# A fixed order for every operation, and layer 1's result kept in DRAM, in an attention kernel with two feed-forward layers

## The chip, the cores and the metric

The kernel runs on one core of a Trainium2 chip, as one program in one launch. The metric is the device time of that program in microseconds (us), lower is better. The kernel before takes 837.86 us (median of 3 runs, 836.62 to 838.67). The profile shown here is of one further execution, which took 837.84 us.

## The reference

```python
def _attn_ref(q, k, v):                      # (4, 8, 576, 64) each
    scores = scale * q @ k^T                 # scale = 1/sqrt(64)
    mask_local   = (rel >= 0) & (rel < 32)                    # heads 0 to 3
    mask_strided = (rel >= 0) & (pos_k % 32 == pos_q % 32)    # heads 4 to 7
    scores = where(mask, scores, -1e9)
    attn = exp(scores - max); attn = attn / (sum(attn) + 1e-9)
    return attn @ v
def _moe_ref(x, w_in, w_out):                # w_in 512 x 2048, w_out 2048 x 512
    h = x @ w_in; g = maximum(0.01 * h, h); return g @ w_out
def _moe2_ref(x, w_in, w_out):
    h = x @ w_in; g = maximum(h, 0) + log1p(exp(-abs(h))); return g @ w_out
x = attn_out.transpose(0, 2, 1, 3).reshape(2304, 512)
return _moe2_ref(_moe_ref(x, w1_in, w1_out), w2_in, w2_out)
```

The four weights reach the kernel as 8-byte floats (2 MiB for a quarter of one), and the result has to be close to float32.

## The kernel before, in words

Both layers multiply in float16, with every operand split into a high and a low half: three products (`mm3`, L676 to L678) stand for one. A weight quarter is loaded with one DMA (L170) into one of four staging areas of `pair`, and then goes through a chain on the vector engine (DVE) and the scalar engine (ACT): largest value (L179), low words (L185), the sign (L224), a shift or scale (L230, L234), the join of two words (L245), high half (L253), low half (L260, on DVE for the first quarter of W1, on GpSimd, that is POOL, for its other three).

**Attention** goes by batch (b = 0 to 3) and six steps ("halves") of a batch: scores on TensorE (PE; `dots`, L397 to L409), maxima on DVE (L436, L447), exponentials on ACT (L477, L499), sums, a reciprocal, a product on POOL (L525), a transpose (on PE for batches 0 and 1, by a DMA, L579, for 2 and 3, followed by a join on DVE, L585), the product with v (L606, L611), and the split of the result into the halves of x (L660 to L672). The largest value of v (L327 or L338) is spread to all partitions by a tiny matmul (`over`, L142).

**Layer 1** goes by 8 units of 288 tokens (u = 0 to 7, two to a batch). `plan_first` makes the gated values g of a unit: 16 column tiles f of W1, each 12 matmuls of 288 columns (one tile is the unit of PE work in this text), then a bend and a split on ACT and POOL (L697 to L703). `plan_second` multiplies g with O1 (16 steps of 12 matmuls) and moves the result (`out_move`, L1080) to a buffer x2 in on-chip memory that holds all of layer 1's output, two arrays of `x2p`. The first unit goes by f (`plan_second_by_f`). The homes of g: `gtile` and `gtile3` are one buffer each; unit 6 and unit 7 both use `gtile`, so that unit 7's g can only be made when the second product of unit 6 is done.

**Layer 2** goes by 9 units of 256 tokens (class `Unit`): the largest value of the unit's x2, a factor, the split (`high`, `rest`), then 8 pairs k of column tiles: `first` (24 matmuls of 256 columns), `size`, `relu`, `soft` on ACT, `add` on POOL (L1421), `sums` on DVE (L1429), the split (`cut_high` L1433 on ACT, `cut_rest` L1437 on DVE) and `second` (21 matmuls; 7 products for 8 in the manner of Strassen). The unit's result is combined on DVE and stored. The O2 quarters, of which the differences are also needed (`o2_sums`, L1249), all go through staging area 1, one after the other.

**The order.** The program first lists 1800 and some operations with `plan.add(engine, cost, function, deps, rank, take, free, behind, port)`, and then `Plan.run` emits them. Each engine executes its own instructions in the order in which they are emitted, so an instruction that waits holds up all that stand behind it on its engine; the DMA triggers of the sync engine (SP) are such a queue too. `run` keeps a model clock for each engine. At each step it takes the engine with the earliest possible start, and of its operations that could start within SLACK the one with the lowest rank (table RANKS, a start and a slope for each kind of work). Buffers that several operations share are counted by name (`take`, `free`): two PSUM pairs "mm", one "sc", and so on. Where the model sees PE idle in the first 130 us, it puts filler matmuls (`idle`, L109) there.

Of the kernel before, what the change touches and what calls it, by code (L numbers as in the profile page):

```python
# [20 lines left out]
P = 128  # L21
# [24 lines left out]
RING = 5  # L46

RANKS = {
# [10 lines left out]
}  # L59
# [12 lines left out]
def build(tc, qt, kl, ks, v, wi1, wo1, wi2, wo2, mloc, mstr, msml, out):  # L72
    nc = tc.nc
    with ExitStack() as ctx:
# [14 lines left out]
        gp3 = pool("gp3", bufs=1)  # L89
        front = ctx.enter_context(ExitStack())  # L90
# [187 lines left out]
        class Attn:  # L278
            def __init__(self, b):

                self.b, self.mode, self.small = b, MODES[b], b in SMALL
                self.q, self.k = {}, {}
                self.ps, self.sm, self.st, self.sv, self.s = {}, {}, {}, {}, {}
                self.turned, self.hl = b in TURNED, {}
# [12 lines left out]
            def load_early(self):  # L297
                for p, masks in ((0, [(mn, msml)]), (1, [(ml, mloc), (ms, mstr)])):
# [4 lines left out]
                    for mask in masks:  # L303
                        nc.scalar.dma_start(*mask)
# [257 lines left out]
            def cut(self, half):  # L562
# [4 lines left out]
                self.cuts = [y[:r].rearrange("p (j n w) -> p j n w", j=2, n=n)[:, :, :, :w] for y in both]  # L567
                nc.scalar.activation(self.cuts[0], self.sv[half], AF.Copy)

            def remain(self, half):  # L570
                hi, lo = self.cuts
# [138 lines left out]
        class Op:  # L710
            def __init__(self, eng, cost, fn, deps, rank, take, free, behind, port):
# [3 lines left out]
                self.next, self.missing, self.end = [], 0, None  # L715

        class Plan:


            HOP, SLACK, LOAD = 0.2, 0.5, 2.6  # L720
# [15 lines left out]
            def run(self, order):  # L736
                rank = {o: order[o.rank[0]][0] + order[o.rank[0]][1] * o.rank[1] for o in self.ops}
# [3 lines left out]
                open_ = []  # L741
                for o in self.ops:
                    o.end, o.next, o.places = None, [], []
                for o in self.ops:
                    o.missing = len(o.deps) + len(o.behind)
                    for d in [*o.deps, *o.behind]:
                        d.next.append(o)
                    if not o.missing:
                        open_.append((0.0, o))
                left = len(self.ops)  # L750
                while left:
                    best = {}
                    for ready, o in open_:
                        t = max(ready, clock[o.eng], clock["port"] if o.port else 0.0)
                        want = collections.Counter()
                        for n in o.take:
# [467 lines left out]
        def part_homes(q):  # L1224
# [4 lines left out]
            if q == 1:  # L1229
                return one(a3, 1536), two(more(), 0)  # L1230
# [419 lines left out]
```

## Time and profile before

| | kernel before |
|---|---|
| median of 3 runs | 837.86 us (836.62 to 838.67) |
| profiled execution: its time, its span | 837.84 us, 835.9 us |
| PE busy | 817.7 us (98%) |
| DVE, ACT, POOL busy | 518.4, 523.6, 261.4 us |
| DMA read, written | 50.12 MB, 4.72 MB |

The span runs from the first to the last instruction of the profiled execution; the execution's own time is 1.9 us longer. In a timeline a row gives the start, the time, the engine (SPq is the DMA queue of SP), the line of the kernel, the operation, what it writes and reads, how many instructions were merged, and in brackets the idle time of the engine just before and the operation that ended it. A busy PE can be busy with fillers (L109), so its busy share alone does not tell how much of its work is needed.

### The profile page before, as it was taken

The page shows a single profiled execution, that of the slowest core. Times are in us where ns is not written, and L with a number is a line of the kernel's source. Part 1 is how long each engine was busy: PE and PEld are TensorE (multiplying, and loading weights), DVE is VectorE, ACT ScalarE, POOL GpSimd, SP SyncE. Part 2 cuts the span into 40 slices and gives each one's busy share as a digit, 9 for nine tenths or more (in the row PEclk, how much of TensorE's full clock was granted, in tenths as well). Part 3 has the DMA queues.
Part 4 walks back from the last instruction along what each step waited for, and adds up shares of the span by engine and source line. Part 5 has one row for each costly group of instructions (what it writes and reads, how often), then busy time and mean ns, then how long its engine had stood idle before and what let it go on. Part 6 is the DMA issues. An engine that isn't in the chain of part 4 may idle for free.

```text
span 835.9 us, 18197 instructions
## 1 busy us (share of the span) xinstructions
PE 817.7 (98%) x7622; PEld 676.4 (81%) x7622; DVE 518.4 (62%) x1198; ACT 523.6 (63%) x947; POOL 261.4 (31%) x193
## 2 busy tenths in 40 slices
PE   9998999899999999999999999999999999999997
PEld 5677777677777777777777878888888888888886
DVE  4999879731367134668448766657474746556564
ACT  1788889721457563336446389868677685959591
POOL 1237949730114431003214033313222231313231
PEclk9999999999999999999999999999999999999999
DMA  9952420420226103550220200000000000000000
GB/s 354 417 198 113 169 101 19 97 82 2 62 67 188 20 2 59 203 201 1 102 101 12 91 1 2 26 2 26 2 26 2 26 2 26 5 22 27 2 27 26
DMA packets 30595, 60.79 MB, mean 73 GB/s; under 512 B 20689, under 2 KB 22065, under 8 KB 27953
## 3 DMA queue, kind: packets, MB, share of 16 engines
q1 hardware_dynamic: 29824, 59.17, 21.1%
q8 instruction: 60, 0.98, 0.5%
q10 hardware_dynamic: 688, 0.46, 0.2%
q14 instruction: 23, 0.18, 0.1%
HBM read 50.12 MB, written 4.72 MB: 66 GB/s over the span
## 4 chain that ended last, share of the span: by engine, by line
PE 75%; DVE 15%; DMA 5%; ACT 3%; issue 1%; POOL 0%; SPq 0%; ACTq 0%; DVEq 0%; POOLq 0%
PE o L676 12%; PE o L678 12%; PE o L677 12%; PE h L676 11%; PE h L678 11%; PE h L677 11%; DVE pair L245 3%; DMA pair<-wo_dram 2%; DVE pair L234 1%; DVE m L179 1%; PE ps L409 1%; DVE pair L1249 1%; PE po L611 1%; DMA pair<-wi_dram 1%; DMA pair<-v_dram 1%; DVE s L447 1%
## 5 line engine op out<-in xcount | busy, mean ns | idle before, releaser
L676 PE MATMUL h<-x,w 128*128 128x256 f16 (+1 forms) x1088 | 303.6, 279 | 0.1
L678 PE MATMUL h<-x,w 128*128 128x256 f16 (+1 forms) x1088 | 303.4, 279 | 0.2 <-POOL w L260 0.2
L677 PE MATMUL h<-x,w 128*128 128x256 f16 (+1 forms) x1088 | 303.4, 279 | 0.0
L1421 POOL TENSOR_TENSOR pair<-pair,t 128x512 f32<-128x512 f32 x72 | 96.3, 1341 | 269.1 <-ACT pair L1409 147.9
L703 POOL TENSOR_TENSOR g<-t,g 128x576 f16<-128x576 f32 x64 | 107.8, 1692 | 150.6 <-ACT g L700 150.6
L676 PE MATMUL o<-g,pair 128*128 128x288 f16 x512 | 146.6, 286 | 0.0
L677 PE MATMUL o<-g,pair 128*128 128x288 f16 x512 | 146.4, 286 | 0.0
L678 PE MATMUL o<-g,pair 128*128 128x288 f16 x512 | 146.4, 286 | 0.0
L1437 DVE SCALAR_TENSOR_TENSOR gr<-pair,x2g,gr 128x896 f16<-128x896 f32 x72 | 87.2, 1221 | 69.1 <-ACT gr L1433 69.1
L676 PEld LDWEIGHTS <-w 128*128 128x128 f16 x1088 | 106.4, 98 | 19.9
L678 PEld LDWEIGHTS <-w 128*128 128x128 f16 x1088 | 106.4, 98 | 19.6 <-POOL w L260 0.5
L677 PEld LDWEIGHTS <-w 128*128 128x128 f16 x1088 | 106.5, 98 | 18.7
L1429 DVE TENSOR_TENSOR pair<-pair 128x128 f32<-128x128 f32 x288 | 72.8, 298 | 54.5 <-POOL pair L1421 51.7
L1404 ACT ACTIVATE t<-h,x2s 128x512 f32<-128x512 f32 x72 | 48.8, 678 | 60.1 <-PE h L678 58.9
L525 POOL TENSOR_TENSOR s<-s,sm 128x288 f32<-128x288 f32 (+6 forms) x48 | 45.0, 958 | 132.0 <-DVE sm L520 67.4
L1433 ACT ACTIVATE gr<-pair,x2g 128x896 f16<-128x896 f32 x72 | 73.7, 1034 | 14.9 <-DVE pair L1429 14.8
L697 ACT ACTIVATE t<-h,gs 128x576 f32<-128x576 f32 x64 | 47.1, 736 | 41.4 <-PE h L678 39.3
L676 PEld LDWEIGHTS <-pair 128*128 128x128 f16 x512 | 50.1, 98 | 14.3 <-issue 0.3
L678 PEld LDWEIGHTS <-pair 128*128 128x128 f16 x512 | 50.1, 98 | 12.6
L677 PEld LDWEIGHTS <-pair 128*128 128x128 f16 x512 | 50.1, 98 | 12.1
L676 PEld LDWEIGHTS <-gr 128*128 128x128 f16 x504 | 49.3, 98 | 7.0 <-ACT gr L1433 1.3
L676 PE MATMUL o<-pair,gr 128*128 128x256 f16 x198 | 54.0, 273 | 1.0 <-ACT gr L1433 1.0
(143 smaller groups left out, 1438.7 us busy)
## 6 DMA issues: line engine op xcount, KB each, us to landing
pair<-wi_dram SPq DMA_DIRECT2D x8, 2048.0 KB, 10.8
pair<-wo_dram SPq DMA_DIRECT2D x8, 2048.0 KB, 8.3
out_dram<-pair SPq DMA_DIRECT2D x18, 256.0 KB, 2.2
v<-v_dram SPq DMA_DIRECT2D x2, 1856.0 KB, 16.2
pair<-v_dram SPq DMA_DIRECT2D x2, 1408.0 KB, 7.1
q<-qt_dram SPq DMA_DIRECT2D x6, 288.0 KB, 5.8
k<-kl_dram SPq DMA_DIRECT2D x4, 304.0 KB, 3.5
q<-qt_dram SPq DMA_DIRECT2D x4, 298.0 KB, 6.4
```

The costliest lines, as they stand in the source:

```text
L245: nc.vector.scalar_tensor_tensor(out=f.rearrange("p (s n) -> p s n", s=2), in0=hi, scalar=3, in1=lo, op0=ALU.logical_shift_left, op1=ALU.b ...
L525: nc.gpsimd.tensor_tensor(out=sv, in0=sv, in1=rs, op=ALU.mult)
L676: nc.tensor.matmul(ps, ah, bh, start=first, stop=False)
L677: nc.tensor.matmul(ps, ah, bl, start=False, stop=False)
L678: nc.tensor.matmul(ps, al, bh, start=False, stop=last)
L697: nc.scalar.activation(t, ps, AF.Prelu, scale=gates[f // 4], alpha=0.01)
L703: nc.gpsimd.tensor_tensor(out=g[:, 1, f : f + 2, :], in0=t, in1=g[:, 0, f : f + 2, :], op=ALU.subtract)
L1404: nc.scalar.activation(t, self.ps[k], AF.Prelu, scale=self.sc[:, k // 2 : k // 2 + 1], alpha=-1.0)
L1421: nc.gpsimd.tensor_tensor(out=r, in0=r, in1=self.a[k], op=ALU.add)
L1429: nc.vector.tensor_tensor(out=r[:, o], in0=r[:, x], in1=r[:, y], op=op)
L1433: nc.scalar.activation(self.a[k][:, 0], self.r[k][:, 1:], AF.Copy, scale=self.ag[:, k // 2 : k // 2 + 1])
L1437: nc.vector.scalar_tensor_tensor(out=a[:, 1], in0=self.r[k][:, 1:], scalar=self.ag[:, k // 2 : k // 2 + 1], in1=a[:, 0], op0=ALU.mult, op1 ...
```

## The change

RANKS goes, and with it the choice in `run`: ORDER lists all 1834 operations by the number of their `plan.add` call, in the sequence in which they are emitted. The model clock stays, for the fillers alone. The numbers: 0 to 4 are batch 0's loads, 5 to 104 its attention; 105 to 109 and 110 to 210 the same of batch 1; 211 to 250 the quarters of W1 (10 each: load, largest, over, scale, low, sign, shift, join, high, rest); 251 to 285 O1; 286 to 445 g of units 0 to 3 (40 each, 5 to two tiles); 446 to 463 the second product of unit 0, 464 to 523 those of units 1 to 3 (20 each); 524 to 634 and 635 to 745 the loads and attention of batches 2 and 3; 746 to 985 units 4 to 7 (g and second product, 40 and 20 each); 986 the opening of a buffer; 987 to 1026 W2; 1027 to 1078 O2 (13 each); 1079 a join of scales; 1080 to 1833 the layer 2 units (83 each but the last: load, largest, over, factor, high, rest, scales, then 9 for each k, then move, two combines, store).

Layer 1's result goes through DRAM: `out_move` writes to a small tile "t" (shared with the gates of both layers), a DMA stores it (16 DMAs), and each layer 2 unit loads its 256 tokens back into one of four slots of the first x2 array (9 DMAs). The second x2 array now holds parts of O2 (`more`), in place of `gtile3`, and unit 7's g moves to `gtile3`, so that it only waits for unit 5's second product. The second product of unit 6 accumulates in "sc". The ring `rs` moves to the places of two W1 tiles. The first `first` of layer 2 waits for the second product of unit 6, no more for that of unit 7. Batch 0's first mask is triggered on SP after the two first loads of q, no more between the two loads of k on ACT's queue. The costs in the `plan.add` calls change the model clock alone.

```diff
+ORDER = (
+    0, 9, 10, 11, 12, 8, 13, 14, 1, 15, 19, 2, 25, 41, 26, 42, 16, 3, 27, 4, 17, 43, 28, 18, 20, 57, 21, 211, 5, 44,
+    29, 221, 45, 105, 22, 6, 106, 73, 30, 46, 31, 32, 7, 33, 58, 23, 35, 47, 48, 74, 34, 36, 24, 59, 212, 37, 49, 60,
+    50, 61, 51, 215, 38, 107, 39, 52, 62, 63, 75, 89, 53, 40, 76, 64, 65, 66, 90, 77, 67, 108, 54, 68, 216, 78, 91,
+    55, 56, 69, 92, 213, 79, 214, 80, 93, 83, 70, 71, 81, 115, 82, 222, 94, 231, 72, 95, 96, 217, 84, 85, 86, 116,
+    218, 97, 117, 118, 87, 98, 219, 99, 100, 101, 131, 88, 225, 102, 119, 220, 103, 223, 104, 120, 226, 224, 121, 235,
+    132, 122, 125, 110, 326, 331, 327, 332, 227, 134, 328, 228, 123, 124, 147, 329, 333, 286, 229, 291, 133, 236, 126,
...
-                for p, masks in ((0, [(mn, msml)]), (1, [(ml, mloc), (ms, mstr)])):
+                for p in range(2):
...
-                    for mask in masks:
-                        nc.scalar.dma_start(*mask)
+                nc.sync.dma_start(mn, msml)
+                for mask in ((ml, mloc), (ms, mstr)):
+                    nc.scalar.dma_start(*mask)
...
+                assert sorted(order) == list(range(len(self.ops)))
+                for o in (self.ops[i] for i in order):
+                    assert all(d.end is not None for d in [*o.deps, *o.behind])
+                    t = max([clock[o.eng], clock["port"] if o.port else 0.0] + [d.end + hop(d, o) for d in o.deps])
...
+        x2 = far.tile([P, KC, NT], F32, name="x2")
+        inward = once(lambda: x2a(0, "x2")[:, : 4 * KC * U2].rearrange("p (i c n) -> p i c n", i=4, c=KC))
...
         def out_move(u, m, ps):
-            nc.scalar.activation(x2_at(u * U1, U1)[:, m], ps, AF.Copy, scale=xs[u])
+            for i, y in enumerate(ps):
+                if i % 2 == 0:
+                    t = moving[u, m + i] = tmp.tile([P, 2, U1], F32, name="t", tag="t")
+                nc.scalar.activation(t if len(y.shape) > 2 else t[:, i % 2], y, AF.Copy, scale=xs[u])
+
+        def out_store(u, m):
+            nc.sync.dma_start(x2[:, m : m + 2, u * U1 : (u + 1) * U1], moving.pop((u, m)))
...
-            home, before = {4: (gtile, 1), 5: (gtile3, 3), 6: (gtile, 4), 7: (gtile, 6)}[u]
+            home, before = {4: (gtile, 1), 5: (gtile3, 3), 6: (gtile, 4), 7: (gtile3, 5)}[u]
...
-            s[u] = plan_second(u, g[u], o1, by("M", k + 16), s[2][0])
+            s[u] = plan_second(u, g[u], o1, by("M", k + 16), s[2][0], "sc" if u == 6 else "mm")
...
-        more = once(lambda: gp3.tile([P, NF * U1], F32, name="more", tag="g"))
+        more = once(lambda: x2a(1, "more"))
...
+            def load(self):
+                self.x2 = inward()[:, self.u % 4]
+                nc.sync.dma_start(self.x2, x2[:, :, self.u * U2 : (self.u + 1) * U2])
...
-                    "PE", 2.63, bind(U.first), [xh, xl, w2[k // 2]] + (s[7][0] if u == k == 0 else []), rank("F", k), take=["mm"], behind=last["g1"],
+                    "PE", 2.62, bind(U.first), [xh, xl, w2[k // 2]] + (s[6][0] if u == k == 0 else []), rank("F", k), take=["mm"], behind=last["g1"],
...
-        plan.run(RANKS)
+        plan.run(ORDER)
```

## Rows read from the trace of the kernel before

**Rows 1.** The page: busy time of the engines, with their share of the span.

```profile
PE 817.7 (98%) x7622; PEld 676.4 (81%) x7622; DVE 518.4 (62%) x1198; ACT 523.6 (63%) x947; POOL 261.4 (31%) x193
```

**Rows 2.** Stretches: start:end, length; busy us of PE, PEld, DVE, ACT, POOL; PEclk, DMA, GB/s.

```profile
0.00:46.50 46.50, 43.27 (x555) 28.00 (x555) 33.34 (x77) 23.34 (x79) 7.56 (x18) 1.00 0.96 377
46.50:61.30 14.80, 14.02 (x167) 10.89 (x164) 14.42 (x51) 13.91 (x32) 6.71 (x5) 1.00 0.42 169
61.30:79.90 18.60, 16.50 (x188) 13.05 (x188) 18.50 (x47) 15.06 (x41) 12.38 (x9) 1.00 0.31 114
79.90:117.80 37.90, 37.71 (x466) 29.93 (x467) 28.67 (x77) 32.43 (x95) 30.26 (x20) 1.00 0.36 129
117.80:154.90 37.10, 35.44 (x290) 28.08 (x290) 32.03 (x32) 32.52 (x39) 29.98 (x15) 1.00 0.34 83
154.90:160.00 5.10, 4.12 (x43) 3.13 (x44) 4.96 (x9) 2.05 (x2) 3.26 (x1) 1.00 0.00 0
160.00:302.20 142.20, 140.67 (x1242) 110.36 (x1241) 55.75 (x175) 66.29 (x171) 43.69 (x33) 1.00 0.27 66
302.20:485.00 182.80, 182.01 (x1531) 145.10 (x1529) 117.51 (x224) 84.00 (x125) 34.28 (x26) 1.00 0.25 88
485.00:829.30 344.30, 343.10 (x3145) 307.35 (x3146) 210.20 (x507) 253.63 (x371) 93.32 (x70) 1.00 0.04 14
```

**Rows 3.** Groups by line, PE: all fillers, the eight at the start among them.

```profile
L109 PE MATMUL idle<-idb 128*128 128x512 bf16 x56 | 17.8, 434 | 1.6 <-DVE idb L100 1.6
```

**Rows 4.** Timeline of PE: start, time, line, idle before and what ended it.

```profile
6.55 2.18 PE L404 MATMUL ps<-qk 64*64 64x96 f32 x22 [0.34 <-DMA qk<-kl_dram]
...
35.39 1.25 PE L109 MATMUL idle<-idb 128*128 128x512 bf16 x5
...
46.58 0.30 PE L676 MATMUL h<-x,w 128*128 128x288 f16 x1
...
50.88 0.29 PE L678 MATMUL h<-x,w 128*128 128x288 f16 x1
...
79.96 0.33 PE L404 MATMUL ps<-qk 64*64 64x54 f32 x4 [1.61 <-DVE mx L447]
...
154.88 0.23 PE L142 MATMUL pm<-idb,m 128*128 128x128 bf16 x1 [1.66 <-DVE m L327]
...
485.40 0.28 PE L676 MATMUL o<-pair,gr 128*128 128x256 f16 x1 [0.98 <-ACT gr L1433]
486.59 0.28 PE L678 MATMUL o<-pair,gr 128*128 128x256 f16 x1 [0.79 <-DVE gr L1437]
```

**Rows 5.** Timeline of DVE in the first 85 us.

```profile
14.32 4.01 DVE L327 TENSOR_REDUCE m<-v 128x1 f32<-128x3712 f32 x1
...
42.51 2.29 DVE L260 TENSOR_TENSOR w<-pair,w 128x2048 f16<-128x2048 f32 x1
...
80.88 2.33 DVE L515 TENSOR_SCALAR sm<-sm,ix,gx 128x8 f32<-128x8 f32 x1
```

**Rows 6.** Timeline of POOL.

```profile
79.11 4.08 POOL L260 TENSOR_TENSOR w<-pair,w 128x2048 f16<-128x2048 f32 x1 [4.17 <-ACT w L253]
```

**Rows 7.** The chain that ended last, in order of time, before layer 2's first second product.

```profile
454.18 1.50 DVE w L1271
...
456.39 1.83 DVE more L1271 x2
458.24 8.70 DMA pair<-wo_dram
466.96 2.29 DVE m L179
...
471.40 1.27 DVE pair L234
...
475.45 2.21 DVE pair L245
```

**Rows 8.** DMA issues: size of one and median us from issue to landing.

```profile
out_dram<-pair SPq DMA_DIRECT2D x18, 256.0 KB, 2.2
```

More of the change, by code (lines that the diff above doesn't have):

```diff
@@ L740, in run @@
                 free = {n: [0.0] * c for n, c in self.places.items()}
[L741 to L756, printed above, removed]
-                            e = free[n][(used[n] + want[n]) % len(free[n])]
-                            want[n] += 1
-                            t = math.inf if e is None else max(t, e + self.HOP)
-                        if t < math.inf:
-                            best.setdefault(o.eng, []).append((t, o))
-                    first = {e: min(t for t, _ in x) for e, x in best.items()}
-                    eng = min((e for e in ("PE", "DVE", "ACT", "Pool", "SP") if e in first), key=first.get)
-                    t, o = min(
-                        (x for x in best[eng] if x[0] <= first[eng] + self.SLACK), key=lambda x: (rank[x[1]], x[0], x[1].index)
-                    )
-                    cost = o.cost
-                    n = int((t - clock[eng] - 0.15) / self.IDLE) if eng == "PE" and t < self.idle_to else 0
+                hop = lambda d, o: (
+                    self.LOAD if d.eng == "SP" else self.HOP if d.eng != o.eng else 0.13 if d.eng in ("DVE", "ACT") else 0.0
+                )
@@ L876, in plan_attention @@
             if b in SUMMED:
-                A.read = step("ACT", 3.3 if A.small else 2.8, lambda half: A.sums(), [ld["v"]], 1)
+                A.read = step("ACT", 3.62 if A.small else 2.8, lambda half: A.sums(), [ld["v"]], 1)
                 big = step("DVE", 0.1, lambda half: A.larger_sum(), [A.read], 1)
@@ L1056, in plan_first @@
                 else:
-                    mm = first = step("PE", 1.473, lambda p=products: p(0), after + [w[f // 4]], take=["mm"])
+                    mm = first = step("PE", 1.473, lambda p=products: p(0), after + [w[f // 4]], take=["mm"], behind=[x[0] for x in out[:1]])
                     more = step("PE", 1.473, lambda p=products: p(1), [mm])
@@ L1105, in plan_second @@
                 if m % 2:
[L1106 to L1109 removed]
+                    y = plan.add(
+                        "ACT", 0.62, lambda m=m, st=st: out_move(u, m - 1, [st["ps"]]), last, rank(4 * m + 3),
+                        take=["t"], free=start,
+                    )
+                    out.append(plan.add("SP", 0.9, lambda m=m: out_store(u, m - 1), [y], rank(4 * m + 3), free=[y]))
             return last, out
@@ L1133, in plan_second_by_f @@
                     start = last
-            return last, [plan.add(
-                "ACT", 1.6, lambda: [out_move(u, m, pss[m]) for m in range(KC)], last, rank(NF), free=start
-            )]
+            y = plan.add("ACT", 1.6, lambda: out_move(u, 0, pss), last, rank(NF), take=["t", "t"], free=start)
+            return last, [plan.add("SP", 1.8, lambda: [out_store(u, m) for m in (0, 2)], [y], rank(NF), free=[y])]
         A, A1 = at[0], at[1]
@@ L1313, in x_at @@
             return t[:, 0], t[:, 1]
-        def pieces(u):
-            t, end, out = u * U2, (u + 1) * U2, []
-            while t < end:
-                n = min(end, (t // (2 * S) + 1) * 2 * S) - t
-                out.append((x2_at(t, n), slice(t - u * U2, t - u * U2 + n)))
-                t += n
-            return out
+        rs = once(lambda: [flat(wpa.tile([P, 4, QW], F16, name="rs", tag=f"a{i}3")) for i in range(2)])
         def w2_join():
@@ L1501, in build @@
             highs.append(xh)
-            xl = plan.add("DVE", 1.2, U.rest, [xh], rank("X", 0), port=True)
-            scaled = plan.add("DVE", 1.13, U.scales, [xl, joined], rank("X", 0))
+            xl = plan.add("DVE", 1.2, U.rest, [xh], rank("X", 0), port=True, free=[ld])
+            scaled = plan.add("DVE", 1.2, U.scales, [xl, joined], rank("X", 0))
             for k in range(NK):
@@ L1526, in build @@
                 g2 = plan.add(
-                    "PE", 2.3, bind(U.second), needs, rank("S", k), take=[] if k else ["sc", "pt", "po"], free=[high],
+                    "PE", 2.293, bind(U.second), needs, rank("S", k), take=[] if k else ["sc", "pt", "po"], free=[high],
                 )
```

158 lines of the change are left out of this document (66 added, 92 removed), and 91 rows, old and new, of tables (ORDER, RANKS).

## The prediction

> **What bounds the kernel now.** Read the page first, then the stretches, then TensorE's (PE's) timeline, and the vector engine's (DVE's) beside it. PE is busy for 817.7 of 835.9 us [rows 1], so no other engine bounds the whole; what an order can win is PE's 18.2 us of idle time and the fillers, which count as busy. The stretches place the idle time, length less busy [rows 2]: 3.2 us before 46.5, 5.0 from there to 160, 1.5 from 160 to 302, 0.8 to 485, 1.2 in layer 2; the last 5.7 us lie behind 829.3, where PE has finished and the output is combined and stored. Of the 56 fillers [rows 3] eight fill the time until the first loads land; the other 48 stand between operations, five of them in 1.25 us [rows 4], that is (1.25 - 0.434) / 4 = 0.20 us each, near 10 us, nearly all before 46.5. An ideal order would thus save some 18.2 - 5.7 - 1.6 (the start) + 10 = 21 us.
>
> Most of that can't be had. Layer 1 starts at 46.58 [rows 4], and until then PE only has attention to do, whose pace DVE sets: 33.3 busy us in 46.5 [rows 2], with little idle once the first scores are there, and the low half of W1's first quarter at 42.51 to 44.80 [rows 5] is nearly its last step before layer 1. From 46.5 to 80 DVE is still full (32.9 of 33.4), and PE loses 2.9 us there; then PE is full until 154.88, where it stands for 1.66 us before the small matmul of batch 2's v [rows 4], and near 1 us more before 160 [rows 2]. The last stall is at 485.4 and 486.6, 0.98 + 0.79 us, at layer 2's first second product [rows 4].
>
> A unit of PE work is a tile of 12 matmuls: 36 matmuls run from 46.58 to 50.88, 35 steps in 4.30 us [rows 4], so 1.474 us a tile.
>
> **The change part by part.** The sum is made against the profiled execution, 837.84 us, which is at the median of the runs (837.86). Each term is what PE loses now less what it loses then.
>
> *First loads.* The trigger of the mask leaves the place between the two k loads on ACT's queue. Now PE waits 0.34 us, until 6.55, for the second k [rows 4]. It can come earlier by the time of a trigger, under half a us, and the mask later by as much. The first scores only start the DVE chain, and the hole that the new order leaves in DVE (the third step's maxima, 42, wait for scores, before 5, the largest value of v) takes it back. I take 0, bounds +0.5 and -0.5.
>
> *Until layer 1 (0 to 46.6).* Read by its numbers, ORDER gives DVE the same work before the last split of batch 0 (104) as now, less the scales of W1's second quarter (224, ten small instructions, about 1.2 us), which come behind it. I followed PE, ACT and DVE by hand through this list with the durations of this trace: every exponential, transpose and copy is ready when DVE comes to its user, so DVE stays full, and the low half of W1 (220) ends near 45.8. The first product (326) starts then and not at 46.58: 0.7 us gained. Bounds: 3 us gained (all idle time of this stretch but the start, and some fillers), 1 lost (a wait of a us that I overlooked, of the size of those of rows 4).
>
> *Layer 1's first 32 tiles (46.6 to 117.8).* Both orders end this stretch with O1's small matmul (264) and have the same PE work before it, but ORDER alternates units 1 and 0 (326, 331, 327, 332, ...), so that one quarter of W1 feeds eight tiles, 11.8 us. PE now loses 0.8 + 2.1 + 0.2 us [rows 2] and two fillers, 3.5 us. By the same hand count the new order waits for "sc" before 147 (0.7 us), for 112's value (0.1) and for ACT's bend before 302 (1.1): 1.9 us. So 1.6 gained; bounds 3.5 gained and 2 lost. The row to weigh is a scalar operation of DVE that takes 2.33 us at 80.88 [rows 5], while POOL makes a low half until 83.19 [rows 6]: the two share something, and a new pairing can cost DVE that again. The Trainium skill (SBUF — State Buffer, "SBUF: two separate sides") says that the port pair which DVE and GpSimd share is an exclusive lock, held for the whole instruction; it speaks against an order that puts three low halves on POOL beside a full DVE. By that rule each of the three could block DVE for all of POOL's 4.08 us: 3 x 2 us more than the row shows, 5.9 less 6, so no gain at all, inside the second rival. By the row it is about 2 us a time, which the order now pays too, and the sum stays. I go by the row.
>
> *The stall at 154.88.* In ORDER batch 2's `over` (530) comes behind 27 tiles of units 3 and 2, and four more stand between its product (547) and O1's use. v's load is triggered behind O1.1's low half as now, near 137; it landed 8 us later in this trace's chain for a 2 MiB load (8.7, [rows 7], as bound), DVE needs 3 us more (149), and PE comes to 530 near 155. Now the same wait costs 1.66 + 0.98 us [rows 2, 4]: 2.6 gained, and what is late next is O1's last low half (285, near 170) before the twelfth step of unit 0's product (458, near 178): hidden. Bounds 2.6 gained, 1 lost.
>
> *160 to 485.* PE loses 2.3 us now [rows 2]. In ORDER the attention of batches 2 and 3 has 10 tiles and more between scores and product, so 1.0 gained; bounds 2.3 gained, 4 lost, since the weights' chain runs here (last rival).
>
> *Start of layer 2.* Now unit 7's second product is all done before the first `first`. The chain into the stall is O2's last quarter: load at 458.24, largest value until 469.25, ready at 486.5 [rows 4, 7], 17.3 us after the small matmul. In ORDER DVE also makes both low halves of that quarter in between (1076, 1078; 1.50 + 1.83 us [rows 7]), less the next unit's scales (1.7 us): 19 us. PE then has nine tiles (973, 976 to 983) and five `first` (1087 to 1123) behind 1068: 9 x 1.474, and 24 matmuls of 256 columns scaled by columns from the tile, 2.62 each, 26 us. So the stall goes, 1.8 us, with 7 us of cover. I take 1.5; bounds 1.8 gained, 1 lost.
>
> *Layer 1's result through DRAM.* 16 stores and 9 loads, 4.7 MB each way. A 256 KB store lands in 2.2 us [rows 8]; taking the load alike, the way there and back is under 5 us, and two stages of PE work lie between for all but the last units, whose results have all of layer 2 before them. The DMA engines are a quarter busy or less there [rows 2]. Cost 0 on PE. The triggers stand in SP's queue ahead of weight loads and the DMA transposes, and a load of x2 that waits for its store holds these up: 2 to 3 us each time, with the cover that the last rival counts. Bounds 0.2 gained (the two-piece unit goes) and 2 lost. The moves, now into "t", compete with the gates for three places: 0, and at most their 16 x 0.1.
>
> *Waits that a hand count doesn't see.* Those of now that no single cause explains (79.96, 485.40 and the like) are around 1 us each; I put 1.5 us for new ones, bounds 0 and 6.
>
> Sum: -0.7 - 1.6 - 2.6 - 1.0 - 1.5 + 1.5 = -5.9, so 837.84 - 5.9 = 831.9, say 832.
>
> **The rivals.** *All of it.* The search behind such a list could remove nearly every wait after 46.5: 3.5 + 2.6 + 2.3 + 1.8 and 3 us in the attention, 13 us, 825. For: each stall has a place of its own. Against: DVE is full until 80, which bounds the first 3 us and most of the next 3.5.
>
> *The stalls only move.* PE's waits of now lie where DVE was late against a model; a new list, made with a model too, is late in other places: the gains of the first two parts and half of the others go, -1.5 to +1, 836.5 to 839. For: DVE's full stretch, and the 2 us of rows 5. Against: the two clear stalls (154.88 and 485.4) have long cover in ORDER. That the list doesn't do what it says is hardly possible, since each engine runs in the order of emission, and it would end here too.
>
> *The weights' chain is late (slower).* W2 and O2 come through areas 1 and 3 one after the other: load, prepare, free, load; and PE's small matmuls (999, 1009, 1019, 1029, 1042, 1055, 1068) stand at fixed places among the tiles. ORDER leaves between them 10, 4, 14, 5, 24, 23 and 21 tiles. Take the third: behind 1009 DVE has two scalings, a low half, scales, a join and a low half (2 x 1.27 + 1.1 + 1.1 + 2.2 + 2.3 = 9.3 us), the load 8.7, the largest value 2.3 [rows 5, 7]: 20.3 against 14 x 1.474 = 20.6. Counted so the covers are about 1.7, 1.9, 0.3, 1.5, 3, 4 and 3 us. Stores and x2 loads ahead of the weights in SP's queue, and ACT between two steps, come out of these. If each link is 4 us longer than counted, PE waits 2.3 + 2.1 + 3.7 + 2.5 + 1 + 0 + 1 = 12.6 us, and the time is 837.84 - 5.9 + 12.6 = 844.5. It decides from some 3 us a link (1.3 + 1.1 + 2.7 + 1.5 = 6.6) on. Against: PE now loses only 0.8 us from 302 to 485 [rows 2] with the same chain.
>
> **How the numbers follow.** Forecast (829 to 835.3) 0.55; all of it (823.5 to 829) 0.12; the stalls only move (835.3 to 839) 0.20; the weights' chain (839 to 847) 0.13. A difference under 0.3%, 2.5 us, is what a measurement of this kernel can't tell from none. Faster by more (under 835.3): 0.55 + 0.12 + a quarter of the third, 0.72. Slower by more (over 840.4): nearly all of the last, 0.12. The rest is 0.16. The range leaves out about a tenth on either side: 826 to 840.
>
> **What would show it.** Right: the first layer 1 product near 45.8; O1's small matmul near 115.5; no wait over 0.5 us before batch 2's `over`, nor at the first second product of layer 2; PE idle about 12 us in the span, with as many fillers before layer 1 as now. Wrong: a first product at 47 or later; waits of PE on DVE's largest values (L179's successor) between 300 and 480; SP's queue holding a weight load behind a load of x2; DVE's small operations longer beside POOL than now.

## The result, and the profile after

The kernel after takes 824.68 us (median of 4 runs, 823.78 to 825.54) against 838.26 (836.62 to 839.12) for the kernel before on the same chip: ratio 0.984, 95% interval 0.982 to 0.986. It is 13.6 us faster, where 5.9 were forecast; 824.7 lies under the range (826 to 840), on the first rival, "all of it" (825). The profiled execution took 824.21 us, its span is 822.4.

The page's busy line and the stretches of the kernel after, to hold against [rows 1, 2]:

```profile
PE 809.0 (98%) x7606; PEld 674.1 (82%) x7606; DVE 512.6 (62%) x1195; ACT 517.4 (63%) x946; POOL 252.6 (31%) x193
```
```profile
41.70:56.40 14.70, 13.35 (x140) 10.35 (x138) 14.63 (x37) 13.30 (x29) 4.84 (x3) 1.00 0.66 273
56.40:75.00 18.60, 18.60 (x227) 15.07 (x226) 17.38 (x69) 17.82 (x52) 17.70 (x12) 1.00 0.40 148
75.00:110.30 35.30, 35.30 (x453) 27.68 (x451) 23.00 (x77) 27.30 (x81) 25.13 (x18) 1.00 0.44 155
110.30:145.00 34.70, 33.42 (x275) 26.58 (x273) 24.74 (x27) 25.06 (x29) 18.13 (x11) 1.00 0.17 50
160.00:300.00 140.00, 140.00 (x1279) 110.52 (x1278) 69.11 (x218) 75.28 (x202) 48.76 (x39) 1.00 0.37 94
300.00:471.00 171.00, 171.00 (x1411) 137.59 (x1410) 104.55 (x159) 73.03 (x81) 29.01 (x19) 1.00 0.30 109
471.00:815.80 344.80, 344.24 (x3158) 308.42 (x3157) 213.36 (x510) 250.16 (x367) 93.64 (x70) 1.00 0.07 22
```

PE's busy column equals the length from 56.4 to 110.3 and from 160 to 471: where the kernel before lost 2.1 + 0.2 us and 1.5 + 0.8 us in the matching stretches [rows 2], nothing is lost (0.6 of the 0.8 is the beginning of the stall that ends at 485.40). What is left stands in PE's waits (what waited, for what, us in total, times, longest), here of the kernel after:

```profile
PE idle L187 <- DVE idb L178: 1.6, 1, 1.6
PE h L755 <- ACT t L776: 1.3, 1, 1.3
PE h L757 <- DVE w L338: 1.3, 1, 1.3
PE ps L476 <- DMA qk<-msml_dram: 1.1, 1, 1.1
PE pt L617 <- POOL s L604: 0.8, 2, 0.4
PE pt L624 <- ACT a L638: 0.7, 3, 0.3
PE o L755 <- ACT pair L1503: 0.6, 1, 0.6
```

The list has thus three waits of its own behind the first loads (L338 is the low half of a weight, L776 the bend of the gates, L1503 the last unit's move) and 40 fillers in place of 56. Their places in PE's timeline, and what the trip through DRAM shows among the DMA issues:

```profile
41.57 0.29 PE L755 MATMUL h<-x,w 128*128 128x288 f16 x1
...
43.23 0.30 PE L757 MATMUL h<-x,w 128*128 128x288 f16 x1 [1.25 <-DVE w L338]
...
120.61 0.28 PE L755 MATMUL h<-x,w 128*128 128x288 f16 x1 [1.27 <-ACT t L776]
```
```profile
x<-t SPq DMA_DIRECT2D x16, 288.0 KB, 4.4
x<-x SPq DMA_DIRECT2D x9, 512.0 KB, 4.5
```

The first tile starts at 41.57 and stops after two matmuls; counted without the 1.4 us that it then stands, layer 1 starts at 42.98. A wait in brackets is 0.16 or 0.17 us short of what PE loses: matmuls start every 0.12 us but are recorded with 0.29, so the end of one hides the first part of a stall. The losses below are taken from the starts. Against the prediction's terms, both profiled executions:

| stretch | forecast | measured | read from |
|---|---|---|---|
| first loads | 0 | 0 | experiments e2, e3 |
| until layer 1 | -0.7 | -3.6 | 46.58 [rows 4] to 42.98 |
| first 32 tiles | -1.6 | -3.8 | 71.1 to 67.3 us, up to O1's small matmul (117.7, 110.3) |
| stall at 154.88 | -2.6 | -3.0 | the stalls at 154.88 and 158 are gone |
| 160 to 485 | -1.0 | -2.6 | five stalls of 0.25 to 1.09 gone |
| start of layer 2 | -1.5 | -2.1 | both stalls gone |
| new waits | +1.5 | +2.2 | 1.44 at 120.6, 0.73 at 814 |
| sum | -5.9 | -12.9 | PE's end: 830.2 to 816.7, -13.5 |

The 0.6 us between the sum and PE's end lie in none of the stalls; where, was not looked for.

### The profile page after: what moved, and what is told of

It is laid out like the page before. It is cut to its first block, busy times and chain, and to the rows that moved or that the text cites. A ratio compares the mean times of both kernels' runs of the same rounds, so it can differ in the third digit from the quotient of the medians.

```text
span 822.4 us, 18203 instructions
## 1 busy us (share of the span) xinstructions
PE 809.0 (98%) x7606; PEld 674.1 (82%) x7606; DVE 512.6 (62%) x1195; ACT 517.4 (63%) x946; POOL 252.6 (31%) x193
## 4 chain that ended last, share of the span: by engine, by line
PE 93%; DVE 4%; DMA 2%; issue 1%; ACT 0%; SPq 0%; DVEq 0%
PE h L755 15%; PE h L757 15%; PE h L756 15%; PE o L755 14%; PE o L757 14%; PE o L756 14%; PE ps L488 1%; PE po L690 1%; DMA v<-v_dram 1%; PE po L685 1%; DMA qk<-msml_dram 1%; DVE pair L312 1%; PE ps L483 1%; DVE m L406 0%; PE pt L617 0%
## 5 line engine op out<-in xcount | busy, mean ns | idle before, releaser
L1458 POOL TENSOR_TENSOR rs<-rs,t 128x512 f32<-128x512 f32 x72 | 96.2, 1338 | 271.8 <-ACT rs L1446 158.4
L782 POOL TENSOR_TENSOR g<-t,g 128x576 f16<-128x576 f32 x64 | 96.2, 1516 | 178.8 <-ACT g L779 178.7
L1466 DVE TENSOR_TENSOR rs<-rs 128x128 f32<-128x128 f32 x288 | 76.2, 307 | 73.8 <-POOL rs L1458 71.3
L1474 DVE SCALAR_TENSOR_TENSOR gr<-rs,x2g,gr 128x896 f16<-128x896 f32 x72 | 84.2, 1174 | 46.4 <-ACT gr L1470 46.2
L1470 ACT ACTIVATE gr<-rs,x2g 128x896 f16<-128x896 f32 x72 | 74.0, 1034 | 35.8 <-DVE rs L1466 35.6
L776 ACT ACTIVATE t<-h,gs 128x576 f32<-128x576 f32 x64 | 46.9, 736 | 51.8 <-PE h L757 46.3
L604 POOL TENSOR_TENSOR s<-s,sm 128x288 f32<-128x288 f32 (+6 forms) x48 | 47.9, 1016 | 98.4 <-DVE sm L599 63.5
L755 PE MATMUL o<-w,gr 128*128 128x256 f16 x216 | 58.9, 273 | 0.6 <-ACT pair L1503 0.6
L757 PE MATMUL o<-w,gr 128*128 128x256 f16 x216 | 58.9, 273 | 0.0
```

The lines of the kernel that those rows point to most:

```text
L604: nc.gpsimd.tensor_tensor(out=sv, in0=sv, in1=rs, op=ALU.mult)
L755: nc.tensor.matmul(ps, ah, bh, start=first, stop=False)
L757: nc.tensor.matmul(ps, al, bh, start=False, stop=last)
L776: nc.scalar.activation(t, ps, AF.Prelu, scale=gates[f // 4], alpha=0.01)
L782: nc.gpsimd.tensor_tensor(out=g[:, 1, f : f + 2, :], in0=t, in1=g[:, 0, f : f + 2, :], op=ALU.subtract)
L1458: nc.gpsimd.tensor_tensor(out=r, in0=r, in1=self.a[k], op=ALU.add)
```

## The experiments

**1. The greedy choice in place of the list, with everything else of the change.**

```diff
-        plan.run(ORDER)
+        plan.run(RANKS)
...
```


> The kernel after with ORDER taken out: its homes, its DRAM trip, its first loads and its model costs stay, and the order is chosen as before, by RANKS. Theory A (the order itself gives the gain): little or nothing is left of the 13.6 us, 835 to 841, since RANKS was fitted to the old homes and costs. Rival B (the new homes and the DRAM trip give the gain, by freeing buffers): 824 to 830.

The left-out part puts the choice of the kernel before back into `Plan.run`. 899.3 us, ratio 1.0743 (1.0724 to 1.0762), beyond both expectations: one wait of 24.8 us on a batch's largest value of v, 115 fillers. Without the list nothing is left of the gain, but what ruins the choice isn't told apart here, since the costs have changed too. So the costs alone, in the kernel before:

```diff
-                    ld[n] = plan.add("SP", 4.6 if A.small else 3.4, ...
+                    ld[n] = plan.add("SP", (4.6 if b else 5.5) if A.small else 3.4, ...
-            sums = step("DVE", 2.5, lambda q=q: o2_sums(q), [y], 0.5)
+            sums = step("DVE", 3.6, lambda q=q: o2_sums(q), [y], 0.5)
...
```


> The kernel before, choosing by RANKS, with the costs that the plan.add calls of after have; nothing else of the change. Theory: RANKS was fitted to the old costs, so the choice falls apart with any others, and that is the larger part of the 61 us by which after's buffers and costs with RANKS (899.3) were slower than before: 860 to 900. Rival: the costs change a per cent or two of the model clock and the choice hardly; then 834 to 845, and the 61 us come from the new operations and homes, for which RANKS has no fitted place.

916.2 us, ratio 1.0945 (1.0909 to 1.0980), beyond the expectation, and with the same longest wait (waits of PE):

```profile
PE pm L142 <- DVE m L327: 24.9, 1, 24.9
```

Some fifteen costs, changed by 44% at most, cost 78 us when the choice goes by them in the kernel before. So the 61 us of the first run say nothing against the new homes; what those would do under the old costs was not run.

**2. The first loads**, alone in the kernel before, and turned back in the kernel after.

```diff
-                for p, masks in ((0, [(mn, msml)]), (1, [(ml, mloc), (ms, mstr)])):
+                for p in range(2):
...
+                nc.sync.dma_start(mn, msml)
```


> The kernel before with the new first loads alone (mask on SP's queue). In the profile of after PE starts its first scores at 6.29 us at full pace (24 matmuls in 1.26 us); in that of before it starts at 5.01 and needs 2.18 us for 22, and fillers run at 0.43 us each until 10.3. Theory A: the new loads bring this, the DVE chain begins 1.6 us earlier and PE's first layer 1 product with it: 1.0 to 1.7 us faster than before. Rival B: the pace of the first 10 us changes from run to run, whatever the loads, or DVE takes it up: within 0.5 us of before.

> The kernel after with batch 0's first mask triggered where the kernel before has it, between the two loads of k on the scalar engine's queue. Theory: the order of the first loads is worth nothing here as it was worth nothing in the kernel before, since DVE's chain bounds the first 41 us; 824 to 825.5, first product 41.5 to 43. Rival: with the new list the loads are what lets DVE start early; then all of the 3.6 us won until layer 1 goes back, 827.5 to 828.5, and DVE's first maxima come later.

839.31 us, ratio 1.0013 (0.9999 to 1.0027); and 823.39 us (0.9831, 0.9806 to 0.9856), first product at 41.85. No difference clear of the noise either way: this step was right.

**3. The first part alone, and the rest alone.** The kernel before with the list's 354 operations up to O1's small matmul (264), then RANKS; and the kernel after with the old sequence up to there, then ORDER (an operation that can't go yet at its place is emitted as soon as it can).

```diff
+                    if forced:
+                        want = self.ops[forced.popleft()]
```


> The kernel before, whose operations up to the small matmul of O1 (number 264) are emitted in ORDER's sequence; the rest is chosen by RANKS as before. Theory A: the first 110 us give 7.4 us of the 13.6 (this matmul came at 110.3 instead of 117.7), and they keep: 830 to 832. Rival B: the rest needs its own list to use it (RANKS then meets buffers and DVE work in another state), and most is given back: 834 to 839.

> The kernel after, whose operations up to the small matmul of O1 are emitted in the sequence of the kernel before (first operation that can go, in the list's sequence, where the two don't fit); the rest follows ORDER. Theory A: the rest gives 6 of the 13.6 us: 831 to 834. Rival B: the rest fits only behind its own first part, and new waits take most of it: 835 to 840.

The first: 861.68 us, ratio 1.0300 (1.0281 to 1.0320), beyond both expectations. O1's small matmul comes at 111.6, so the first part works without the new homes, but RANKS then loses more than it had (waits of PE):

```profile
PE h L694 <- ACT t L715: 21.7, 1, 21.7
```

The second: 831.30 us, ratio 0.9938 (0.9920 to 0.9957). From O1's small matmul to PE's end it takes 705.0 us, against 712.4 before and 706.4 after. (Its profiled execution took 2.1 us more than the other three, and the granted clock was 0.97 from 46.5 to 110, so its first part shows 121.4 where the others must have had near 119.3.) So the later half of the gain, 6.0 us, comes without the first (but with the new homes); the first, 7.4, did not last with RANKS behind it.

**4. What the first product waited for.** Batch 1's second scores (131) and the maxima that free their area (118) put back behind W1's low half (220), as the kernel before has them.

```diff
-    218, 97, 117, 118, 87, 98, 219, 99, 100, 101, 131, 88, 225, 102, 119, 220, 103, 223, 104, 120, 226, 224, 121, 235,
+    218, 97, 117, 87, 98, 219, 99, 100, 101, 88, 225, 102, 220, 118, 119, 103, 223, 104, 131, 120, 226, 224, 121, 235,
```


> The kernel after with one place of the list turned back to what the kernel before does: batch 1's second step of scores (131), and the maxima that free their PSUM area (118), stand behind the low half of W1's first quarter (220) instead of ahead of it. Theory: in the kernel before the first layer 1 product waits for these scores, not for W1's low half; the list's gain until layer 1 comes from having them out of the way. Then the first product starts near 44.9 us (low half ready 43.1, maxima 0.6, scores 1.2) against an effective 43.0 now, and O1's small matmul is 1 to 1.9 us late (111.3 to 112.2, now 110.3); time 825.5 to 826.6. Rival: the low half alone decides; first product within 0.5 us of 43.0 and the time within 0.6 us of 824.7.

825.62 us (825.22 to 825.71; ratio 0.9856, 0.9832 to 0.9880), 1.7 and 2.2 us above two kernels with the list unchanged on the same chip (points 2 and 6). PE's timeline of this kernel, and of the kernel before just ahead of the row at 46.58 [rows 4]:

```profile
43.20 1.26 PE L483 MATMUL ps<-qk 64*64 64x96 f32 x24
44.39 0.30 PE L755 MATMUL h<-x,w 128*128 128x288 f16 x1
```
```profile
45.39 1.26 PE L404 MATMUL ps<-qk 64*64 64x96 f32 x24 [0.35 <-DVE mx L447]
```

The first product comes 1.4 us later than the effective 42.98, and O1's small matmul 1.0 to 1.3 us later (111.6; 110.3 to 110.6 with the list unchanged). As expected: in the kernel before too the low half was ready (44.80) and the product stood behind scores that waited for DVE's maxima. (In experiment 4 eight fillers, which the model puts there, run from 41.38 until the scores start, so no wait is recorded; the maxima end at 43.02.)

**5. What bounds the first product in the list.** The low words of W1's second quarter (225) behind the low half (220); then also unit 3's second bend (413) ahead of O1's sign (267).

```diff
-    ... 101, 131, 88, 225, 102, 119, 220, 103, 223, ...
+    ... 101, 131, 88, 102, 119, 220, 225, 103, 223, ...
-    324, 325, 408, 409, 416, 267, 417, 256, 413, 414, ...
+    324, 325, 408, 409, 416, 413, 417, 256, 267, 414, ...
```


> The kernel after with one operation of its list moved: the low words of W1's second quarter (225, 1.20 us of DVE) stand behind the low half of the first quarter (220) instead of ahead of it. Theory: DVE has next to no idle time from v's largest value to that low half (0.24 of 28.5 us) and PE waits 1.4 us for it, so what stands ahead of it on DVE moves PE one for one: low half ends near 42.0, PE's wait falls from 1.4 to 0.3 us, O1's small matmul 1.1 us earlier (109.2), time 823 to 824. Rival: DVE is as full behind the first product, so the operation is paid there (a wait for the second quarter's halves or for batch 1's maxima between 46 and 75): O1's small matmul within 0.4 us of 110.3, time within 0.6 us of after's.

> The kernel of e12_low_words_behind with one more operation moved: the bend of unit 3's second pair of gates (413) stands on ACT's queue ahead of O1's sign (267), which waits there for DVE until 117.8 us. Theory: PE's wait of 1.3 us at 119 to 120.6 is this queueing and goes, with nothing late behind it since O1's chain has cover until unit 0's second product: 1.3 us less than e12, 821.5 to 823. Rival: the sign 0.7 us later makes O1's first quarter late, or the next bend (418) then waits: less than 0.5 us from e12.

825.17 us (0.9846, 0.9821 to 0.9870) and 823.75 us (0.9827, 0.9804 to 0.9850). The theory failed in the first and the rival's time held: PE waits less for the low half but stops once more (waits of PE):

```profile
PE h L757 <- DVE w L338: 0.9, 1, 0.9
PE h L756 <- DVE x L751: 0.8, 1, 0.8
```

and DVE's timeline says why:

```profile
40.07 2.29 DVE L338 TENSOR_TENSOR w<-pair,w 128x2048 f16<-128x2048 f32 x1 [0.65 <-ACT w L331]
42.28 1.22 DVE L263 TENSOR_SCALAR pair<-pair 128x2048 uint32<-128x2048 uint32 x1
43.42 0.58 DVE L751 TENSOR_TENSOR x<-po,x 128x108 f16<-128x108 f32 x3
```

The low half could not start before ACT had made the high half, so DVE now stands 0.65 us there, and the moved operation (42.28) stands ahead of the last split of batch 0, which the next matmul needs. O1's small matmul came no earlier (111.9, in an execution whose clock fell, see the last section; 111.4 in the second). In the second kernel the wait for the bend is gone; it misses its 821.5 to 823 by what the first move did not bring. Point 8 has the bend alone.

**6. The stores of the trip through DRAM, doubled.** Every store of layer 1's result is issued twice, the second to a tensor that nothing reads.

```diff
+            nc.sync.dma_start(x3[:, m : m + 2, u * U1 : (u + 1) * U1], moving.pop((u, m)))
```


> The kernel after with every store of layer 1's result made twice, the second to a DRAM tensor that nothing reads: 16 more triggers on SP's queue and 4.7 MB more written. Theory: the trip through DRAM is hidden, DMA engines are a quarter busy or less and no PE wait ends on it; within 1 us of 824.7. Rival: SP's queue is tight (weights, transposes, stores and loads of x2 in one queue) and each further trigger holds up a weight's load: PE waits for largest values between 300 and 480 us, 2 us or more in all, 827 or above.

823.95 us (0.9834, 0.9807 to 0.9862), the same waits but for 0.4 us on a load of k at the start. The stores are hidden, and no wait of PE in the list above ends on a load of x2, so "cost 0 on PE" was right.

**7. What the trip buys: the home of unit 7's gated values.** First the old home in the kernel after; then the kernel before with its old homes, the list and the new costs. In both an operation that can't go yet at its place is emitted as soon as it can.

```diff
-            home, before = {4: (gtile, 1), 5: (gtile3, 3), 6: (gtile, 4), 7: (gtile3, 5)}[u]
+            home, before = {4: (gtile, 1), 5: (gtile3, 3), 6: (gtile, 4), 7: (gtile, 6)}[u]
-                for o in (self.ops[i] for i in order):
+                    o = next(x for x in left if can(x))
```


> The kernel after with unit 7's gated values back in the buffer that unit 6 uses, so that they can only be made behind unit 6's second product; operations that are not yet possible at their place in the list are emitted as soon as they are. Theory: the own home is what gives PE tiles to do while O2's last quarter and unit 6's moves are made; without it PE waits once for the bend of unit 7's last gates and once at layer 2's first second product (0.98 + 0.79 us before) and near 1 us elsewhere: 826.5 to 830. Rival: the list has cover in layer 2's first products anyway and the home is worth nothing: within 1 us of 824.7.

> The kernel before (layer 1's result in on-chip memory, unit 7's gated values in unit 6's buffer, first loads as before) with the list of after, the operations that store and load the result left out of it, and operations that are not yet possible at their place emitted as soon as they are. Theory: the list needs the home that only the trip through DRAM makes free; without it PE waits as with the old home of unit 7 in the list of after (839.3), in the weights' chain between 400 and 460 us, and the first layer 2 product waits for unit 7's result besides: 838 to 843, with the first part up to O1's small matmul as fast as after's (near 110.3). Rival: it is the trip's buffers and triggers in the list that made the old home dear there; the list alone gives most of the gain, 824 to 831.

839.32 us (1.0020, 1.0003 to 1.0038; median of 12 executions, one of which took 2468 us for a reason that isn't known, the others 838.6 to 841.1) and 848.41 us (1.0113, 1.0092 to 1.0135): both lose the whole gain and more, and both expectations were too low (826.5 to 830; 838 to 843). The first part is untouched (O1's small matmul at 109.6 and 109.8). The loss of the first kernel is between 400 and 460 us. Its waits there, and the chain into the longest:

```profile
PE pm L210 <- DVE m L247: 7.3, 1, 7.3
PE h L745 <- ACT t L766: 2.5, 1, 2.5
```
```profile
420.85 1.91 ACT L1315 ACTIVATE w<-pair 128x2048 f16<-128x2048 f32 x1 [17.77 <-PE h L746]
422.79 2.29 DVE L1319 SCALAR_TENSOR_TENSOR w<-pair,w 128x2048 f16<-128x2048 f32 x1 [25.63 <-ACT w L1315]
425.11 0.35 SPq L238 DMA_DIRECT2D pair<-wo_dram  x1
432.93 2.29 DVE L247 TENSOR_REDUCE m<-pair 128x1 f32<-128x2048 f32 x1 [7.85 <-DMA pair<-wo_dram]
```

The same four steps in the kernel after:

```profile
398.49 1.91 ACT L1314 ACTIVATE w<-pair 128x2048 f16<-128x2048 f32 x1 [2.77 <-PE h L756]
400.43 2.29 DVE L1318 SCALAR_TENSOR_TENSOR w<-pair,w 128x2048 f16<-128x2048 f32 x1 [5.37 <-ACT w L1314]
404.49 0.35 SPq L248 DMA_DIRECT2D pair<-wo_dram  x1
412.15 2.29 DVE L257 TENSOR_REDUCE m<-pair 128x1 f32<-128x2048 f32 x1 [7.69 <-DMA pair<-wo_dram]
```

Read from the top: the halves of an O2 quarter go into the place of a W1 tile, so ACT waits for PE's last tile of unit 7 that reads it. With its own home unit 7's g is made early, and the place comes free at 398; in the old home it comes behind unit 6's second product, and the place comes free at 420.9. The next O2 quarter then lands 20.8 us later, and PE, out of tiles, stands 7.4 us. Without the trip x2 fills both arrays, parts of O2 lie where unit 7's g now lies, and there is no own home: the second kernel waits 8.9 us for largest values of weights and 4.1 us for a move of layer 1's result. This is the chain of the prediction's last rival, and the change's part that keeps it from coming true. It is not worth 15 us by itself: the kernel before had the old home, an order that suited it, and lost 0.8 us in the stretch from 302 to 485 [rows 2].

**8. The one wait that the list brought, taken away.** Unit 3's second bend (413) ahead of O1's sign (267), alone, and the kernel after once more beside it.

```diff
-    324, 325, 408, 409, 416, 267, 417, 256, 413, 414, ...
+    324, 325, 408, 409, 416, 413, 417, 256, 267, 414, ...
```


> The kernel after with one operation moved: the bend of unit 3's second pair of gates (413) ahead of O1's sign (267) on ACT's queue. Theory: PE's wait of 1.27 us at 120.6, which the new list brought, is queueing behind the sign alone; it goes and nothing is late behind it: 1.2 to 1.4 us less than after on the same chip, near 823.2, with PE busy for all of 110 to 145. Rival: what e13 won there is given back later when the first product is not moved as well: within 0.5 us of after.

> The kernel after once more, on the chip of e14_bend_first_alone and for comparison with it: 823.5 to 825.5.

822.57 us (822.10 to 824.01; 0.9821, 0.9798 to 0.9843) against 823.81 (823.44 to 824.46): 1.2 us less in the medians, though single runs overlap. The profiles agree with it. ACT's timeline in the kernel after, then in this one:

```profile
117.80 2.13 ACT L318 ACTIVATE pair<-pair 128x2048 f32<-128x2048 f32 x1 [2.79 <-DVE pair L312]
119.83 0.73 ACT L776 ACTIVATE t<-h,gs 128x576 f32<-128x576 f32 x1
```
```profile
116.39 0.74 ACT L776 ACTIVATE t<-h,gs 128x576 f32<-128x576 f32 x1 [1.48 <-PE h L757]
117.71 2.15 ACT L318 ACTIVATE pair<-pair 128x2048 f32<-128x2048 f32 x1 [0.58 <-DVE pair L312]
```

In the kernel after the sign stands at the head of ACT's queue for 2.79 us, waiting for DVE, while a bend that PE needs stands ready behind it. Turned round, the sign starts when it did and the bend comes for nothing; PE is busy for all of 110 to 145. This version has the lowest median of all that were run.

**9. Without the fillers between operations.**

```diff
-                            self.idle(n, y)
...
+                            pass
```


> The kernel after without the 32 fillers between operations (the 8 at the start stay). Theory: the fillers only fill time in which PE waits for DVE before the first layer 1 product, so without them the time is the same within 0.7 us of after, and idle time stands in their place; they cost nothing and the 16 fewer of them in after were no part of the gain. Rival 1: they stand in the way of PE's own work, 0.2 us each, and 1 to 3 us are won. Rival 2: the granted clock falls while PE has only attention to do, and PE's 20 us of work before 41 us take longer: 3 us or more lost, with a granted clock under 1.00 in that stretch.

825.22 us (0.9846, 0.9820 to 0.9871), but of four executions two took 824.1 and 824.3 and two 826.2 and 827.6. The two lower ones are the theory. The profiled one (826.2) has the granted clock at half just before layer 1 (last section), so something like the second rival is seen in it, later than it says, and at 2.0 us above the two lower executions and not 3. Whether the fillers keep the clock up isn't settled by four executions.

## Why the prediction was wrong

**The failed step is the hand count through the list**: "DVE stays full, and the low half of W1 (220) ends near 45.8. The first product (326) starts then and not at 46.58", and by "the same hand count" 1.9 us of waits in the first 32 tiles. The low half ended at 43.17. The step had three faults, and the first two can be read in the trace of before.

DVE was not full. DVE's stretch from the start of v's largest value to the end of the low half, in the kernel before and then after (length, busy):

```profile
14.32:44.80 30.48, 28.87 (x65) 1.00 1.00 413
```
```profile
14.65:43.17 28.52, 28.28 (x61) 1.00 1.03 426
```

The stretch took 30.48 us with 1.6 idle; the list leaves 0.24 idle and 0.6 less busy time. I had taken "little idle" from the busy share of the whole 46.5 us.

The low half was not the gate. It was ready at 44.80 in the kernel before; the product stood behind scores that waited for DVE. Experiment 4 shows that this place alone is worth 1.4 of the 3.6 us until layer 1. The rest, 2.2 us, goes with DVE's stretch, which is 2.0 us shorter; no run turns that part back alone.

Recorded durations on DVE can't be added, those of short instructions least. In DVE's timeline of the kernel after a maximum and its read are recorded with 0.25 + 0.08 us, and the next starts 0.18 us after the first:

```profile
35.84 0.25 DVE L526 CUSTOM_DVE_ANT_0 s<-ps,qk 128x96 f32<-128x96 f32 x1
36.02 0.08 DVE L526 DVE_READ_ACCUMULATOR2_ANT mx<- 128x1 f32 x1
36.02 0.25 DVE L526 CUSTOM_DVE_ANT_0 s<-ps,qk 128x96 f32<-128x96 f32 x1
```

The rows give 0.33 us recorded for 0.18 taken. The Trainium skill (VectorE: DVE Perf Modes, "The DRAIN you can't avoid") lets the next instruction wait until the one ahead has left the pipeline, and says that one which isn't held starts earlier; these rows are of the second kind. Over the whole stretch above, the rows of the kernel after add up to 32.9 us in 28.3 us of busy time. I added durations, so the new order came out later by my count than it is (how much of the 2.6 us from 45.8 to 43.17 each fault makes isn't told apart), and the counted waits (for "sc" before 147, for the bend before 302) are not in the trace. The wait for a bend that did come, at 120.6, is another one, which I hadn't followed.

**The other steps.** First loads, and the trip at no cost on PE: right, points 2 and 6, though the way there and back took 4.4 + 4.5 us where I took under 5. The stall at 154.88: right in place and size (-3.0 for -2.6). Start of layer 2: right in place, 0.6 more. 160 to 485: right in place, mis-sized: all of it went, 2.6 us, where I took 1.0 with a bound of 2.3. The bound was misread: 0.6 of it belongs to the stall at 485.40, which the next term counts again; the five stalls of the stretch have 1.7 us in the busy column, and about 0.16 us of each is hidden there. New waits: right in size (2.2 for 1.5). A term that wasn't there: the own home of unit 7's values, told in the change and given no price; experiment 7 shows that the list hangs on it. Two readings that enter no term were off as well: the idle time from 46.5 to 160 is 5.7 us by [rows 2], not 5.0, and PE's end is at 830.2, not 829.3.

**The port pair.** The prediction weighed the Trainium skill's rule (SBUF — State Buffer, "SBUF: two separate sides") of an exclusive lock shared by DVE and GpSimd, by which three low halves on POOL would have cost the gain, against the one row of 2.33 us at 80.88 [rows 5]. In the kernel after, DVE's rows beside these low halves (at 53.65, 72.48 and 85.78) keep their length; POOL's and DVE's timeline at the first:

```profile
53.65 4.22 POOL L338 TENSOR_TENSOR w<-pair,w 128x2048 f16<-128x2048 f32 x1 [4.17 <-ACT w L331]
53.84 2.25 DVE L257 TENSOR_REDUCE m<-pair 128x1 f32<-128x2048 f32 x1
56.01 0.24 DVE L526 CUSTOM_DVE_ANT_0 s<-ps,qk 128x96 f32<-128x96 f32 x1
```

These two kinds aren't hit, so the low halves didn't cost the gain, and the 2 us of the row at 80.88 weren't paid beside any of the three. The Trainium skill (the same section) limits the lock to some kinds of DVE instructions, and these two are not among them; the trace agrees.

Such time is paid elsewhere, which the prediction didn't count. Of DVE's rows in the kernel after, 35 are over 0.2 us longer than the shortest of the same line and shape, and every one of them lies beside a row of POOL; up to 160 us they are 9.6 us longer in all. (In the kernel before it is 32 rows, each beside one of POOL, and 17.8 us.) Two of them stand ahead of the sign in point 8: first the chain that ended last in the kernel after, then POOL's timeline beside it, then DVE's timeline where this line runs with no row of POOL beside it:

```profile
113.37 4.41 DVE pair L312 x2
```
```profile
111.95 2.52 POOL L782 TENSOR_TENSOR g<-t,g 128x576 f16<-128x576 f32 x2 [4.29 <-ACT g L779]
115.09 1.59 POOL L782 TENSOR_TENSOR g<-t,g 128x576 f16<-128x576 f32 x1 [0.63 <-ACT g L779]
```
```profile
418.87 1.29 DVE L312 TENSOR_SCALAR pair<-pair,s 128x2048 f32<-128x2048 f32 x1
```

The two take 4.41 us, where two like the last would take under 2.6: by this estimate the sign could have started 1.8 us earlier, so the wait of 1.4 us at 120.6 comes as much from the work beside POOL as from the order of ACT's queue. How much of the gain, or of what is left, lies in such rows was not run.

**The chances.** "All of it" was put at 0.12, against it DVE's full stretch until 80. Up to the low half DVE had 1.6 us of waits in that stretch: that was the part to measure before it was counted as a bound. The time came out at this rival's number, and mostly for its reason: all stalls of the kernel before behind 46.5 went, and new ones of 2.2 us came. The last rival (weights' chain) has the right mechanism and needs the old home to come true.

## What to carry to other kernels

A full engine's stretch is a bound only as long as its own idle time in just that stretch is subtracted; and when the first instruction of a stage starts later than its last input is ready, look at what stands ahead of it on its own queue. Look too at what runs beside a row that is longer than others of its kind. An in-order queue loses most where an instruction waits at its head for a slow producer while one that is ready stands behind: here one such exchange gave 1.2 us. A buffer moved out of on-chip memory at no visible gain may pay elsewhere: ask whose place comes free, and what chain starts from that.

## What the runs showed of the hardware that was not expected

PE's granted clock fell from 1.00 to 0.50, from 2.4 to 1.2 GHz, in single executions for about 3 us, mostly just before or behind the first layer 1 product (in e2's near 20 us, in e5's from 83). PE's stretches (length, busy, granted clock) of the kernel of experiment 9, of e12 and of e14_bend_first_alone:

```profile
41.00:44.00 3.00, 3.00 (x50) 0.50 0.96 401
```
```profile
44.00:47.00 3.00, 2.95 (x13) 0.53 1.08 436
```
```profile
41.00:44.00 3.00, 1.75 (x28) 1.00 0.98 412
```

In the first PE had been busy for 7.17 of the 11 us ahead of it, in the second for 1.28 of 3 us. The third had 1.25 us of idle time at that place and stayed at full speed, as did e13 with the same two stops as e12. A fall costs about 1.5 us (3 us at half speed, an estimate), which is part of why e12 (824.3 to 827.5) and experiment 9 (824.1 to 827.6) spread more than others. In the profiled execution of e12, its slowest, PE also stood 1.7 us more at 214, where a join on DVE took 2.80 us beside POOL and 1.08 in the kernel after. What decides a fall isn't shown here. Behind the 7.4 us stall of experiment 7 the mean granted clock was 0.66 over 5 us (436 to 441), which makes about 1.7 of that kernel's loss.
